# Raw q and k loads moved from SyncE's queue to GpSimd's; three small pieces of work moved in their engines' orders

## The chip, the core and the metric

The kernel runs on one core of a Trainium2 chip (trn2). The metric is the device time in microseconds (us) of one execution; lower is better. The engines are named as the profile names them: PE (TensorE, matmuls), PEld (TensorE's weight loads), DVE (VectorE), ACT (ScalarE), POOL (GpSimd) and SP (SyncE, which only issues DMAs). A "q" behind an engine's name is its sequencer, where DMAs are issued.

## The reference, cut to what matters

```
attention: 4 batches x 8 heads, 576 rows, head_dim 64
  scores = q k^T / 8, causal; plus min(-(cum_i - cum_j), 0), cum = cumsum(max(s, 0))
  x = softmax(scores) v                       -> 2304 tokens x 512
first MLP:   h = max(x w_in, 0);  y = (h*h) w_out      512 -> 2048 -> 512
second MLP:  h = y w_in2;  out = (h cos h) w_out2      512 -> 2048 -> 512
```

The result is wanted in float32. The kernel gets that accuracy from faster formats by splitting a value into a high and a low part and adding three products (high*high, high*low, low*high).

## The kernel before, in words

**Work and stages.** The 2304 tokens of x are cut into 9 blocks of 256 (`NB1`). A block is filled by one or two query segments, each with 8 heads; a head of a segment is a unit of `heads` (96 in all), and its query rows are cut into one or two tiles of up to 128 rows. A tile is a job (160 in all). Units of the early heads (`n < EARLY`, the first 16) take a simpler path. In blocks 3 and 6 the first segment, and in block 8 both, have one tile per head, so every step begins a new head there; elsewhere a head lasts two steps.

The first MLP of block k runs in the same steps as the attention of block k+1. The list `slots` holds its matmul groups in order: (1, chunk) is `g1` (line 857, hidden chunk f of block k: 12 matmuls into `hps`, of which there are two halves), (2, chunk) is `g2` (line 886, 12 matmuls into `y`), two chunks behind. The second MLP comes after the attention, from 612 us on in the trace, and is not touched.

**One step.** `step` (line 990 on) writes out by hand the order in which each engine gets its work. All engines run their own instructions strictly in that order, and wait for each other by semaphores. For step i, with attention and MLP, it is:

1. `x_high`: ACT copies freshly transposed x from PSUM (`xps`) into `xh` (line 668).
2. `load_ext` for the next head (POOL's queue, line 340): the four rows of sums that go under k and q in tile `k2`.
3. The first MLP slot: 12 matmuls. In front of a `g2`, `rests` makes sure that its low part `gl` has been issued (DVE, line 876).
4. `prep_high` (ACT, lines 347 and 348): rounds the raw q and k of the next head into `hi` and `k2`.
5. `evacuate` (DVE): divides a finished pair of heads by their sums into `xp` (line 642).
6. woven together: `softmax_tail` (DVE: mask of tile i-1, line 516; the two halves `p` of tile i-2, lines 561 and 565, then a DMA transpose of `p` on SP, line 571; where the width isn't a multiple of 128, POOL first clears the pad of `p`, line 560), `w_step` (bits of weights) and `v_early` (`v_scale`, lines 405 and 410).
7. `x_low` (DVE, line 674), `rests` (DVE, line 876), `w_lows` (line 750).
8. `act` (ACT, lines 868 to 870): `g` = max(0, h) squared and its high part `gh`.
9. `prep_low` (DVE, lines 355 and 358): the low parts of q and k of the next head. After it the raw tile is free.
10. `emit_qk` (PE, line 502), the other MLP slots, the exponential of tile i-1 (ACT, line 533), `load_v` (SP, line 368).
11. `turn` (PE, line 657): transposes `xp` into `xps`; `v_sums` (PE, line 399); `emit_pv` (PE, line 602).
12. `v_late` (square, high and low parts of v, its load on POOL's queue, its store on SP's), then `load_raw` for the head three ahead (SP, line 221).

**The raw tiles.** `raw` has two buffers. The load for head n waits until `prep_low` of head n-2 has read its buffer, and `prep_high` of head n waits for it to land.

**v.** The values are scaled by a power of two, two heads at a time: 16 groups of `v_load` (line 380), `v_square` (ACT, line 391), `v_sum` (PE: two small matmuls with ones, into other columns of `xps`), `v_scale` (DVE), `v_high` (ACT, line 419), `v_low` (DVE, line 426) and `v_store`. The queue `vq` gives each its step: square in step t, sum in t+1, scale and high in t+2, low and store in t+3. `xps` is one PSUM tile, shared by the sums of v and the transposed x, which lie in different columns.

**Between blocks** there is a step without attention, whose only MLP slot is one group, and then the last x of the block is evacuated and turned. `turn` marks in `xtq` whether a piece is the last of its block.

Of the kernel before, what the change touches and what calls it, by code (L numbers as in the profile page):

```python
# [24 lines left out]
BT = 256  # L25
# [13 lines left out]
def _weave(*chains):  # L39

    chains = [iter(c) for c in chains if c is not None]
    while chains:
        for c in list(chains):
            if next(c, c) is c:
                chains.remove(c)
# [61 lines left out]
DR_BITS = 0  # L107
XST_TO = 20
TURN_FROM = 24
V_STRIDE = 11  # L110
V_NEAR = 6
V_TIME = 7
# [3 lines left out]
def attention_moe_moe_kernel(  # L116
# [18 lines left out]
    nc = tc.nc  # L135
# [59 lines left out]
    for x in range(H // 2):  # L195
        t = wp.tile([128, 2, 2 * BT], F32, tag=f"w{2 * NF - (2, 3, 4, 6)[x]}", name="early")
# [13 lines left out]
    def load_raw(n):  # L210
        nq, nl = heads[n][6], heads[n][8]
        if n < H:
            return
        if n < EARLY:
            t = at.tile([128, KQ], F32, tag=("hi", "k2")[n % 2], bufs=2, name="early1")
            nc.sync.dma_start(out=t[0:64, 0:2 * BT], in_=qk[n, 0:64, 0:2 * BT])
            nc.sync.dma_start(out=t[64:66, 0:2 * BT], in_=c1_d[n - H])
            hd[n] = t
            return
        raw = at.tile([128, KQ], F32, tag="raw", bufs=2, name="raw")  # L220
        nc.sync.dma_start(out=raw[:, BT - nq:BT + nl], in_=qk[n, :, BT - nq:BT + nl])
        hd[n] = [None, None, raw]

    def v_own(b):
# [29 lines left out]
    def store_ones(eng, n0, n1):  # L254
# [10 lines left out]
        out=mask[:, 512:640], in_=mask[:, 512:640], pattern=[[-1, 128]], compare_op=ALU.is_ge,  # L265
# [4 lines left out]
        out=ident, in_=ident, pattern=[[-1, 128]], compare_op=ALU.not_equal, fill=1.0,  # L270
# [3 lines left out]
    for t in early[2:]:  # L274
        early_ones(t, nc.gpsimd)
    nc.vector.tensor_scalar(
        out=cs[0:32, 0:S], in0=cs[0:32, 0:S], scalar1=0.0, scalar2=8.0, op0=ALU.max, op1=ALU.mult
    )
    cc = []
    for x0, x1, t in ((0, BT, "xh"), (BT, S, "xl")):  # L280
        nc.vector.tensor_tensor_scan(
            out=c8[0:32, x0:x1], data0=cs[0:32, x0:x1], data1=cs[0:32, x0:x1],
# [27 lines left out]
    for x in range((XST + 1) // 2):  # L310
        t = wp.tile([128, 2, 512], F32, tag=f"w{2 * NF - 5 - x}", name="xst")
# [18 lines left out]
    evq, xtq, xcq = [], [], []  # L330
# [107 lines left out]
    def v_early():  # L438
        for f, g in vq[0] if vq else ():
            if f is v_scale:  # L440
                yield from f(g)

    def v_sums():
        for f, g in vq[0] if vq else ():
            if f is v_sum:
                f(g)
# [7 lines left out]
    def v_steps(gs, start):  # L454
# [9 lines left out]
        for x, due in enumerate(at):  # L464
            at[x] = max(0, min(due, free))
            free = at[x] + V_STRIDE
        return at

    def v_add(gs, at, stored=True):

        for g, t in zip(gs, at):
            fs = []
            if g not in vs:
                fs, t = [(t, v_load)], t + 2
            fs += [(t, v_square), (t + 1, v_sum), (t + 2, v_scale), (t + 2, v_high), (t + 3, v_low)]
            for x, f in fs + [(t + 3, v_store)] * stored:
                vq.extend([] for _ in range(x + 1 - len(vq)))
                vq[x].append((f, g))
# [171 lines left out]
    def turn(held):  # L650
        while xtq and (held > 0 or xtq[0][-1]):
            held -= 1
            k, c, rws, o, xp, _ = xtq.pop(0)
            pt = xps[:, 0:BT]
            m = 0
            for ti, r in enumerate(rws):
                nc.tensor.transpose(pt[:, m:m + r], xp[0:r, ti, :], ident[0:r, 0:r])  # L657
                m += r
            xcq.append((k, c, o, m, pt))

    def x_high():
        for k, c, o, m, pt in xcq:
            if k not in xb:
                xb[k] = (
                    m1.tile([128, KD, BT], F32R, tag="xh", bufs=2, name="xh"),
                    m1.tile([128, KD, BT], F32R, tag="xl", bufs=2, name="xl"),
                )
            nc.scalar.copy(xb[k][0][:, c, o:o + m], pt[:, 0:m])

    def x_low():  # L670
        while xcq:
            k, c, o, m, pt = xcq.pop(0)
            xh, xl = xb[k]
            nc.vector.tensor_tensor(  # L674
                out=xl[:, c, o:o + m], in0=pt[:, 0:m], in1=xh[:, c, o:o + m], op=ALU.subtract
            )
# [3 lines left out]
    nraw, next_, nhigh, nlow = [2], [0], [0], [0]  # L680

    def upto(cnt, n, f):
        while cnt[0] < min(n, NH):
            f(cnt[0])
            cnt[0] += 1

    def job(i):
        return jobs[i] if 0 <= i < NJ else None
# [4 lines left out]
    def heads_ahead(i, *fs):  # L693
        if job(i) and jobs[i][1] == 0:
            for cnt, f, d in fs:
                upto(cnt, jobs[i][0] + d, f)
# [263 lines left out]
    g2done = [0]  # L960
# [6 lines left out]
    def moe_slot():  # L967
        part, n = slots.pop(0)
        k, f = chunks[n]
        if part == 1:  # L970
            w_need(2 * f + 1)
            g1(k, f)
            return n
        w_need(2 * f + 2)
        rests(n)
        g2(k, f)
        g2done[0] += 1
        if k == NB1 - 1 and 2 * f >= RAWS:
            w_load(2 * (NF + f))
            w_load(2 * (NF + f) + 1)  # L980
            nw[0] = max(nw[0], 2 * (NF + f + 1))
# [14 lines left out]
    def softmax_tail(i):  # L996
        if job(i - 1):
            yield from emit_mask(i - 1)
        for j in stage(2, i - 2):
            yield from emit_split(j)  # L1000

    def step(moe=0, bits=0, attn=True):

        i = prog[0]
        held = len(xtq)
        prog[0] += attn
        if attn:
            for j in stage(1, i - 2):
                emit_exp(j)
        x_high()  # L1010
        if attn and job(i - 2):
            emit_turn(i - 2)
        if attn:
            heads_ahead(i, (next_, load_ext, 2))
        w_age()
        w_scales()
        n = moe_slot() if moe else None
        if attn:
            heads_ahead(i, (nhigh, prep_high, 2))
        _weave(evacuate())  # L1020
        y_evict()
        if not attn:
            rests()
        _weave(softmax_tail(i) if attn else None, w_step(bits), v_early())
        x_low()
        rests()
        w_lows()
        if attn and job(i - 1) and jobs[i - 1][0] < EARLY:
            for j in stage(1, i - 1):
                emit_exp(j)  # L1030
        act(n)
        if attn:
            heads_ahead(i, (nlow, prep_low, 2))
        if attn and job(i):
            emit_qk(i)
        for _ in range(moe - 1):
            act(moe_slot())
            y_evict()
        w_sums()
        if attn:  # L1040
            for j in stage(1, i - 1):
                emit_exp(j)
        if attn:
            for j in stage(0, i - 2):
                if jobs[j][1] == 0:
                    load_v(jobs[j][0])
        turn(held if moe and i > last_job[0] + TURN_FROM else len(xtq))
        v_sums()
        if attn:
            for j in stage(3, i - LAG[0]):  # L1050
                if j > i - lag(j):
                    stages[3] -= 1
                    break
                emit_pv(j)
        w_ahead()
        v_late()
        if attn:
            heads_ahead(i, (nraw, load_raw, 4))
        if later and prog[0] >= later[0][0]:
            later.pop(0)[1]()  # L1060

# [17 lines left out]
    def w_age():  # L1079
        wsum.extend(wsq)  # L1080
        wsq.clear()
# [18 lines left out]
    def w_lows():  # L1100
        while wlow:
            w_lo(wlow.pop(0))

    def w_step(n):

        js = list(range(nw[2], min(nw[2] + n, wlim[0])))
        while wlow:
            w_lo(wlow.pop(0))
            yield
        w_squares()  # L1110
        while wrest:
            w_rest(wrest.pop(0))
        if js:
            w_clip_to(js[-1])
            for _ in zip(*[w_bits(j) for j in js]):
                yield
            for j in js:
                if wq[j][0] == 0:
                    wrest.append(j)
                else:  # L1120
                    wbit.append(j)
            nw[2] += len(js)
# [18 lines left out]
    def w_need(j):  # L1141

        w_stats(j)
        while wrest and wrest[0] < j:
            w_rest(wrest.pop(0))
        while wlow and wlow[0] < j:
            w_lo(wlow.pop(0))
# [10 lines left out]
    while prog[0] < unit_done(0):  # L1158
        i = prog[0]
# [3 lines left out]
    for k in range(NB1):  # L1163
# [6 lines left out]
        last = len(slots) - nslots  # L1170
        J = goal - start + 1 if goal > start else NF
        for i in range(J):
            bits = 0
            if k == 0:
# [3 lines left out]
                bits = int((i + 1) * B0_BITS) - int(i * B0_BITS)  # L1178
            if k == NB1 - 1:
# [16 lines left out]
                bits = min(2 * GROUPS[0][1], int(max(0, i - 1) * B8_BITS)) - int(max(0, i - 2) * B8_BITS)  # L1196
                bits = max(0, bits)
            n = len(slots) - last - nslots + math.ceil(nslots * (i + 1) / J)
# [233 lines left out]
```

## Time and profile before

| | |
|---|---|
| median of 3 runs | 996.22 us (994.47 to 996.5) |
| the profiled execution, its own time | 994.47 us |
| its span, first to last instruction | 992.7 us |
| attention and first MLP | 0 to 612 us of the span |
| second MLP | 612 us to the end |
| PE busy over the span | 960.4 us (97%) |
| DVE, ACT, POOL busy | 729.7, 654.2, 162.7 us |

A row of the profile's timeline reads: start in us from the span's start, duration in us, engine, line, operation, output tile <- input tiles, shapes, count; in brackets the idle time of the engine just before, and the instruction or DMA that ended it.

### The profile page before, as it was taken

Reading aid. Unit: us, or ns where it says so; the run is one execution under the profiler, and the core shown is the slowest. Engines: PE = TensorE matmul, PEld = TensorE weight load, DVE = VectorE, ACT = ScalarE, POOL = GpSimd, SP = SyncE. Lnnn points to the kernel's source line nnn. Section 1 sums busy time; section 2 is a strip of 40 time slices with the busy share of each in tenths; the row PEclk is TensorE's granted clock in tenths of the full one; section 3 lists DMA queues with packets and bytes.
Section 4 is the critical chain, followed back from the end, with each engine's and each line's share of the span. In section 5 each row is a group of like instructions: output and inputs, shape, how many; then the busy total and the mean of one; then the engine's idle time right before and its main releaser. Section 6 shows DMA issues by size and latency. Waiting matters only on the chain.

```text
span 992.7 us, 20523 instructions
## 1 busy us (share of the span) xinstructions
PE 960.4 (97%) x7266; PEld 737.9 (74%) x7266; DVE 729.7 (74%) x1865; ACT 654.2 (66%) x1596; POOL 162.7 (16%) x258
## 2 busy tenths in 40 slices
PE   5999899999999999999999999999999999999998
PEld 4788898899999999999999997444444454444444
DVE  6979788878777897777988265898988855545555
ACT  4789776777768777766776586677766543334333
POOL 2000011111111121111110023421043440001101
PEclk9999999999999999999999999999999999999999
DMA  7955589756877886467898579210000000001001
GB/s 262 307 179 182 128 199 204 169 124 161 190 173 163 181 193 169 119 143 156 191 214 177 193 240 357 90 39 1 1 1 1 1 1 1 11 33 43 30 14 64
DMA packets 150711, 126.65 MB, mean 128 GB/s; under 512 B 108048, under 2 KB 125792, under 8 KB 150608
## 3 DMA queue, kind: packets, MB, share of 16 engines
q1 hardware_dynamic: 146688, 119.05, 45.9%
q0 software_dynamic: 3904, 6.29, 2.4%
q8 instruction: 57, 0.93, 0.4%
q14 instruction: 46, 0.38, 0.1%
q10 hardware_dynamic: 16, 0.01, 0.0%
HBM read 85.25 MB, written 15.81 MB: 102 GB/s over the span
## 4 chain that ended last, share of the span: by engine, by line
PE 83%; DVE 8%; ACT 4%; DMA 2%; issue 2%; SPq 0%; DVEq 0%; ACTq 0%
PE hps L857 19%; PE y L886 18%; PE o L1310 18%; PE hp L1255 18%; PE qkp L502 4%; PE pvs L602 4%; DVE wt L750 1%; DMA raw<-in_qk_dram 1%; DVE st L729 1%; DVE sb L516 1%; PE xps L657 1%; ACT sb L533 1%; DMA early<-c 1%; DMA rw<-in_w_dram 0%; DVE k L358 0%
## 5 line engine op out<-in xcount | busy, mean ns | idle before, releaser
L857 PE MATMUL hps<-xh,wt 128*128 128x256 f32 x1152 | 239.5, 291 | 4.1 <-ACT g L868 4.0
L886 PE MATMUL y<-gh,wt 128*128 128x256 f32 x1152 | 236.6, 288 | 0.0
L857 PEld LDWEIGHTS hps<-xh,wt 128*128 128x128 f32 x1152 | 190.2, 192 | 6.6 <-ACT g L868 5.4
L886 PEld LDWEIGHTS y<-gh,wt 128*128 128x128 f32 x1152 | 188.8, 191 | 1.2
L1255 PE MATMUL hp<-yh,wt 128*128 128x512 f16 (+1 forms) x640 | 185.9, 358 | 0.0
L1310 PE MATMUL o<-wt,gh 128*128 128x512 f16 x576 | 171.3, 379 | 1.5 <-ACT wt L1325 1.4
L886 PE MATMUL y<-gl,wt 128*128 128x256 f32 x576 | 162.9, 283 | 1.6 <-DVE gl L876 1.6
L857 PE MATMUL hps<-xl,wt 128*128 128x256 f32 x576 | 163.5, 284 | 0.9 <-DVE xl L674 0.9
L1255 PEld LDWEIGHTS <-wt 128*128 128x128 f16 x960 | 91.9, 98 | 93.0
L1267 ACT ACTIVATE a<-hp,hsc 128x512 f32<-128x512 f32 (+1 forms) x80 | 51.4, 643 | 115.9 <-PE hp L1255 114.5
L868 ACT ACTIVATE g<-hps 128x256 f32<-128x256 f32 x144 | 54.6, 379 | 104.8 <-PE hps L857 103.2
L1255 PE MATMUL hp<-yl,wt 128*128 128x512 f16 (+1 forms) x320 | 114.4, 358 | 0.0
L886 PEld LDWEIGHTS y<-gl,wt 128*128 128x128 f32 x576 | 110.0, 191 | 2.7 <-DVE gl L876 2.2
L857 PEld LDWEIGHTS hps<-xl,wt 128*128 128x128 f32 x576 | 110.8, 192 | 1.4 <-DVE xl L674 1.1
L1310 PE MATMUL o<-wt,gl 128*128 128x512 f16 x288 | 109.2, 379 | 0.0
L1268 DVE TENSOR_SCALAR kf<-a 128x512 f32<-128x512 f32 (+1 forms) x80 | 35.0, 437 | 96.4 <-ACT a L1267 95.7
L1310 PEld LDWEIGHTS <-gh 128*128 128x128 f16 x576 | 56.3, 98 | 66.3 <-issue 1.7
L533 ACT ACTIVATE sb<-sb,nb 128x128 f32<-128x128 f32 (+8 forms) x160 | 93.8, 586 | 11.8 <-DVE nb L516 11.7
L340 POOL DMA_DIRECT2D k<-ext_d x80 | 41.1, 513 | 338.1 <-ACT g L869 103.7
L516 DVE CUSTOM_DVE_ANT_0 sb<-qkp,mask 128x128 f32<-128x128 f32 (+8 forms) x160 | 72.7, 454 | 13.3 <-PE qkp L493 6.9
L1276 ACT ACTIVATE a<-kf 128x512 f32<-128x512 f32 (+1 forms) x80 | 46.8, 585 | 48.3 <-DVE kf L1269 47.8
L876 DVE TENSOR_TENSOR gl<-g,gh 128x256 fp32r<-128x256 f32 x144 | 60.9, 423 | 21.6 <-PE y L886 11.3
(119 smaller groups left out, 1694.8 us busy)
## 6 DMA issues: line engine op xcount, KB each, us to landing
rw<-in_w_dram SPq DMA_DIRECT2D x64, 512.0 KB
raw<-in_qk_dram SPq DMA_DIRECT2D x32, 352.0 KB
raw<-in_qk_dram SPq DMA_DIRECT2D x16, 384.0 KB
v_d<-vt SPq DMA_DIRECT2D x16, 320.0 KB
raw<-in_qk_dram SPq DMA_DIRECT2D x16, 320.0 KB
vb<-v_d SPq DMA_DIRECT2D x32, 160.0 KB
vr<-in_v_dram POOLq DMA_DIRECT2D x15, 320.0 KB, 4.6
y_d<-yst SPq DMA_DIRECT2D x18, 256.0 KB
```

What stands on the lines that cost most here:

```text
L340: nc.gpsimd.dma_start(out=hd[n][1][64:68, BT - nq:BT + nl], in_=ext_d[n, :, BT - nq:BT + nl])
L502: nc.tensor.matmul(p[0:r, 0:cn], m[0:kk, qo:qo + r], m[0:kk, BT + c0:BT + c0 + cn], start=(kk == 128), stop=(kk == 68),)
L516: nc.vector.tensor_tensor_reduce(out=sb[0:r, c0:c0 + cn], in0=p[0:r, 0:cn], in1=mask[0:r, mo + c0:mo + c0 + cn], scale=-0.125, scalar=(3.0 ...
L533: nc.scalar.activation(out=sb[0:r, 0:w], in_=sb[0:r, 0:w], func=ACTF.Exp, scale=-1.0, bias=j["nb"], accum_out=pd[n - h % 2]["z"][0:r, ti, ...
L857: nc.tensor.matmul(hp, w[:, a, c * 128:(c + 1) * 128], (xh, xl)[e][:, c, :], start=(n == 0), stop=(n == 3 * KD - 1),)
L868: nc.scalar.activation(out=g, in_=hp, func=ACTF.Relu)
L876: nc.vector.tensor_tensor(out=gl, in0=g, in1=gh, op=ALU.subtract)
L886: nc.tensor.matmul(yps[k][d // 2][:, d % 2, :], w[:, a, d * 128:(d + 1) * 128], (gh, gl)[e], start=(f == 0 and n == 0 and d % 2 == 0), sto ...
L1255: nc.tensor.matmul(hp, w[:, a, c * 128:(c + 1) * 128], (yh, yl)[e][:, c, :], start=(m == 0), stop=(m == 3 * KD - 1),)
L1267: nc.scalar.activation(out=a, in_=hp, func=ACTF.Copy, scale=sm["hsc"][:, j, f:f + 1], bias=0.25)
L1276: nc.scalar.activation(out=a, in_=kf, func=ACTF.Sin, scale=-6.2831850)
L1310: nc.tensor.matmul(ops[j][a], (gh, gl)[e][:, a * 128:(a + 1) * 128], w[:, x, :], start=(first and m == 0), stop=(last and m == 2),)
```

## The change

- `load_raw` issues on POOL's queue (line 221). Up to step 27 it stays at the step's end; later the same load stands at the start of the next step, just behind `load_ext`. 80 loads are concerned.
- `v_sum` goes to entry t+2 of `vq`, and `v_sums()` stands behind the first MLP slot of a step, no longer between `turn` and `emit_pv`. So the two matmuls of a group move from the end of one step to behind the first group of matmuls of the next.
- `v_early()` (`v_scale`) leaves the woven part and follows `prep_low`.
- While fewer than two `g2` are done, `rests()` is called ahead of `softmax_tail` in steps with attention, too.
- Where the last piece of a block has been turned, `x_low` is called ahead of `softmax_tail`; `turn` passes on the mark for it.

```diff
+RAW_LATE = 28
...
-        nc.sync.dma_start(out=raw[:, BT - nq:BT + nl], in_=qk[n, :, BT - nq:BT + nl])
+        nc.gpsimd.dma_start(out=raw[:, BT - nq:BT + nl], in_=qk[n, :, BT - nq:BT + nl])
...
-            fs += [(t, v_square), (t + 1, v_sum), (t + 2, v_scale), (t + 2, v_high), (t + 3, v_low)]
+            fs += [(t, v_square), (t + 2, v_sum), (t + 2, v_scale), (t + 2, v_high), (t + 3, v_low)]
...
-            k, c, rws, o, xp, _ = xtq.pop(0)
+            k, c, rws, o, xp, last = xtq.pop(0)
...
-            xcq.append((k, c, o, m, pt))
+            xcq.append((k, c, o, m, pt, last))
...
             heads_ahead(i, (next_, load_ext, 2))
+            if i > RAW_LATE:
+                heads_ahead(i - 1, (nraw, load_raw, 4))
         w_age()
         w_scales()
         n = moe_slot() if moe else None
+        v_sums()
...
         y_evict()
-        if not attn:
+        if not attn or g2done[0] < 2:
             rests()
-        _weave(softmax_tail(i) if attn else None, w_step(bits), v_early())
+        done = bool(xcq) and xcq[-1][-1]
+        if done:
+            x_low()
+        _weave(softmax_tail(i) if attn else None, w_step(bits))
         x_low()
...
             heads_ahead(i, (nlow, prep_low, 2))
+        _weave(v_early())
         if attn and job(i):
             emit_qk(i)
...
         turn(held if moe and i > last_job[0] + TURN_FROM else len(xtq))
-        v_sums()
...
         v_late()
         if attn:
-            heads_ahead(i, (nraw, load_raw, 4))
+            if i < RAW_LATE:
+                heads_ahead(i, (nraw, load_raw, 4))
```

## Rows read from the trace of the kernel before

**Rows 1.** The page's first part: busy us (share of the span) and instructions.
```profile
PE 960.4 (97%) x7266; PEld 737.9 (74%) x7266; DVE 729.7 (74%) x1865; ACT 654.2 (66%) x1596; POOL 162.7 (16%) x258
```
**Rows 2.** Timeline of PE: six waits, each with what ended it.
```profile
57.20 0.38 PE L886 MATMUL y<-gl,wt 128*128 128x256 f32 x1 [1.62 <-DVE gl L876]
...
113.79 0.39 PE L857 MATMUL hps<-xl,wt 128*128 128x256 f32 x1 [0.88 <-DVE xl L674]
...
117.27 0.27 PE L399 MATMUL xps<-ss,ones 128*128 128x2 f32 x1 [1.55 <-ACT vt L391]
...
173.13 0.39 PE L857 MATMUL hps<-xh,wt 128*128 128x256 f32 x1 [1.10 <-ACT g L868]
...
183.67 0.27 PE L657 MATMUL xps<-ident,xp 64*128 64x64 f32 x1 [0.54 <-DVE vsc L405]
...
517.27 0.39 PE L857 MATMUL hps<-xh,wt 128*128 128x256 f32 x1 [1.66 <-ACT g L868]
```
**Rows 3.** Timelines of ACT near 57 us and of DVE near 112 us.
```profile
57.24 0.39 ACT L868 ACTIVATE g<-hps 128x256 f32<-128x256 f32 x1 [1.28 <-DVE gl L876]
...
111.84 0.68 DVE L516 CUSTOM_DVE_ANT_0 sb<-qkp,mask 128x512 f32<-128x512 f32 x1
```
**Rows 4.** ACT's waits for raw: who <- whom: us, times, longest; two in the timeline.
```profile
ACT hi L347 <- DMA raw<-in_qk_dram: 15.4, 11, 4.7
...
171.93 0.72 ACT L347 CAST hi<-raw 128x640 fp32r<-128x640 f32 x1 [4.70 <-DMA raw<-in_qk_dram]
...
515.96 0.78 ACT L347 CAST hi<-raw 128x704 fp32r<-128x704 f32 x1 [3.67 <-DMA raw<-in_qk_dram]
```
**Rows 5.** The chain of waits: those raws, issue and us to landing; DVE freeing their buffers.
```profile
166.42 5.43 DMA raw<-in_qk_dram
...
511.01 4.87 DMA raw<-in_qk_dram
...
163.56 0.75 DVE L358 TENSOR_TENSOR k<-raw,hi 64x576 fp32r<-64x576 f32 x1
...
506.56 0.75 DVE L358 TENSOR_TENSOR k<-raw,hi 64x576 fp32r<-64x576 f32 x1
```
**Rows 6.** Line 380, POOL's loads of v: ns min/median/max, landing; POOL and DVE near 170 us.
```profile
L380 POOL DMA_DIRECT2D vr<-in_v_dram x15: 735/752/779, 75.3 to 386.7; - x15
...
DMA to landing us min/median/max: 3.3/4.6/5.9
...
170.74 0.51 POOL L340 DMA_DIRECT2D k<-ext_d  x1 [3.35 <-DVE p L561]
...
170.28 0.45 DVE L561 TENSOR_SCALAR p<-sb 64x576 f16<-64x576 f32 x1
```
**Rows 7.** PE's turns in three steps, DVE's work there, v_scale's group of the lines view.
```profile
202.40 0.27 PE L657 MATMUL xps<-ident,xp 64*128 64x64 f32 x1
...
218.06 0.48 PE L657 MATMUL xps<-ident,xp 128*128 128x128 f32 x2
...
246.40 0.27 PE L657 MATMUL xps<-ident,xp 128*128 128x128 f32 x1
...
202.99 0.42 DVE L358 TENSOR_TENSOR k<-raw,hi 64x256 fp32r<-64x256 f32 x1
...
219.34 0.42 DVE L358 TENSOR_TENSOR k<-raw,hi 64x256 fp32r<-64x256 f32 x1
...
247.14 0.42 DVE L876 TENSOR_TENSOR gl<-g,gh 128x256 fp32r<-128x256 f32 x1
...
L405 DVE TENSOR_SCALAR vsc<-xps 128x2 int32<-128x2 int32 x16 | 2.5, 154 | 5.5 <-PE xps L399 3.4 <-ACT xh L668 2.1
```
**Rows 8.** POOL at the start; a window: us, busy by engine, PEclk, DMA share, GB/s.
```profile
5.56 0.52 POOL L192 MEMSET early<- 2x512 f32 x1
...
8.00:9.00 1.00, 0.00 (x0) 0.00 (x0) 0.00 (x0) 0.00 (x0) 0.00 (x0) 1.00 0.28 105
```
**Rows 9.** The page's group of ACT's first reading of hps (idle before, and its releaser).
```profile
L868 ACT ACTIVATE g<-hps 128x256 f32<-128x256 f32 x144 | 54.6, 379 | 104.8 <-PE hps L857 103.2
```

More of the change, by code (lines that the diff above doesn't have):

```diff
@@ L658, in turn @@
                 m += r
-            xcq.append((k, c, o, m, pt))
+            xcq.append((k, c, o, m, pt, last))
     def x_high():
-        for k, c, o, m, pt in xcq:
+        for k, c, o, m, pt, _ in xcq:
             if k not in xb:
@@ L671, in x_low @@
         while xcq:
-            k, c, o, m, pt = xcq.pop(0)
+            k, c, o, m, pt, _ = xcq.pop(0)
             xh, xl = xb[k]
```

## Prediction

> **What bounds the kernel now.** I read the page first, then PE's waits in its timeline, then what the releasers of those waits were doing on their own engines. The page says that PE is busy 97% of the span [rows 1]: 992.7 less 960.4 leaves 32.3 us in which it does nothing. That is all a change of order can win, and most of it lies where this change doesn't reach (the start before the first matmul, the prolog). So the prediction is a list of single waits of PE, each about 1 us, and the reader is to see in [rows 2] which engine ended each. DVE and ACT have idle time on the whole [rows 1], so their lateness counts only where PE stands waiting for exactly that operation.
>
> **The change part by part.** 0.2% of this kernel is 2.0 us, about what a measurement can tell from no change.
>
> *First low parts.* `rests()` goes ahead of `softmax_tail` for the first two `g2`. It moves DVE's `gl`, one operation per chunk; no DMA moves. PE stood 1.62 us for the first at 57.20 [rows 2]. ACT stood 1.28 us for the same `gl`, because it could not write the next `g` before the old one was read [rows 3]. With `gl` earlier both waits go, and the next thing late is ACT itself, so I take ACT's 1.28; bounds 0 and 1.62. The mask moved behind `gl` has no price, as ACT has its own work ahead of the exponential that follows.
>
> *A block's last x.* `x_low`, one DVE operation, goes ahead of the mask that started at 111.84 [rows 3], and PE stood 0.88 us for it at 113.79 [rows 2], from 112.91 on. Started in the mask's place it ends before PE gets there: 0.88; bounds 0 and 0.88. The other blocks show no such wait, and get nothing. The mask comes later by one short operation that runs beside PE's matmuls.
>
> *v's sums on PE.* Two small matmuls for each of 16 groups. One waited 1.55 us for ACT's squares, in the short step between two blocks at 117.27 [rows 2]. Behind the next step's first group of matmuls the squares are done: 1.55 is won; bounds 0 and 1.55.
>
> *v_scale on DVE, the price.* Two operations, 0.15 us each [rows 7], now come last of DVE's work in their step. Who waits for them? The row at 183.67 shows PE's `turn` standing for `v_scale` [rows 2]: it writes other columns of `xps`, yet it has to wait until `v_scale` has read. So in each step that holds a `v_scale` and a `turn`, PE now waits for all DVE work of that step. Counting steps from the loops, there are three such steps with attention where DVE is the later one (a fourth has two MLP slots ahead of its `turn`, and DVE is done by then). In the first, DVE's last piece ends at 202.99 + 0.42 = 203.41; less 0.30 for the two operations that no longer stand ahead of it, plus 0.15 for the first of them, `v_scale` has read at 203.25, where `turn` started at 202.40: 0.85 lost. In the second, 219.34 + 0.42 - 0.15 = 219.60 against 218.06: 1.55 (about; DVE there waits for ACT's exponential, so nothing ahead of it gets earlier). In the third, without `prep_low`, 247.14 + 0.42 - 0.15 = 247.40 against 246.40: 1.00 [rows 7]. Together 3.4 us, and PE has no idle time near by to take them up; bounds 0 and 4.5, should DVE be a third of a microsecond later in each. Queued behind the waiting `turn` are `emit_pv` and the next step's matmuls.
>
> *Raw loads.* 80 DMAs of up to 384 KB leave SP's queue and stand on POOL's. On SP each stood behind the step's DMA transpose, the load of vb and the store of v; on POOL it stands behind the sums' rows (`load_ext`), which are short. ACT waited 11 times for a raw, 15.4 us in all [rows 4], but only two of those waits were long enough to reach PE, through a late `g`: 4.70 us of ACT gave 1.10 of PE at 173.13, and 3.67 gave 1.66 at 517.27 [rows 2, 4]. Their buffers were free at 163.56 + 0.75 = 164.31 and 506.56 + 0.75 = 507.31, and SP issued them at 166.42 and 511.01 [rows 5]: 2.1 and 3.7 us late. POOL can issue them at once. From issue to landing SP's two took 5.43 and 4.87 us [rows 5]; POOL's loads of v, 320 KB, take 4.6 us, at worst 5.9 [rows 6]. Even with 5.9 the two land 1.6 and 2.7 us sooner. ACT's first wait then shrinks to about 3.1, under the 4.70 - 1.10 = 3.60 that cost PE nothing; the second to about 1.0, under 3.67 - 1.66 = 2.0. I take both in full, 2.76; bounds -4 (they land later, below) and 2.76.
>
> What now queues behind a raw on POOL: while it waits for `prep_low`, the pad of `p`, the next sums' rows and the load of v stand, and DVE's `p` and SP's transpose wait for the pad. A raw's issue costs POOL about 0.75 us, as the loads of v [rows 6]; so the pad is done about 1 us behind `prep_low`, and DVE gets to `p` about a mask later, 0.68 [rows 3]. A few tenths of DVE here and there: 0 to 1, and I take 0.3.
>
> The first raw moves most. POOL's work at the start ends at 5.56 + 0.52 = 6.08 [rows 8], and nothing that this raw needs is missing then, so it is loaded at 6 us instead of 79, amid the loads that PE's first matmul waits for. DMA is only 0.28 busy from 8 us on, at 105 GB/s [rows 8]; at that rate per busy share 384 KB take about 1.0 us. Bounds 0 and 1.0; I take 0.3, nearer the idle window.
>
> [...] The row at 170.74 shows POOL's DMA beginning as DVE's `p` ended (170.28 + 0.45) [rows 6]: an issue on POOL can be held by DVE, up to 0.45 us here. [...]
>
> *The sum.* Won: 1.28 + 0.88 + 1.55 + 2.76 = 6.47. Lost: 3.4 + 0.3 + 0.3 = 4.0. Net 2.5 us. The profiled execution took 994.47 us with a span of 992.7; it becomes 992.0. That execution was the fastest of three, and the median is 1.75 above it, so for the median I take 996.2 - 2.5 = 993.7 us.
>
> **The rivals.**
>
> - *The turns don't wait.* If DVE gets to `v_scale` before PE gets to `turn`, the 3.4 us stay away: 996.2 - 5.9 = 990.3. For it: DVE loses its own waits for the sums, 5.5 us over the 16 groups [rows 7]. Against: in the second of the three steps DVE is held by ACT, not by the sum. Chance 0.18.
> - *The small waits come back.* PE gets past 57, 113 and 117 us sooner and then meets the same ACT and DVE, so 1.28 + 0.88 + 1.55 are given back: 996.2 - 2.76 + 4.0 = 997.4, no change. For it: ACT and DVE are tightest there. Against: ACT and DVE get part of the time, too. Chance 0.17.
> - *v_scale is late for ACT, too (slower).* `v_high` comes in the same step on ACT, which then stands with `prep_high` and `g` behind it. If at the other 13 groups it waits the 1.13 us that the three turns wait on average, and half reaches PE, that is 7.4: 996.2 - 2.5 + 7.4 = 1001.1. It decides from where ACT's wait exceeds its idle time ahead of `g`. Against: ACT waits 103.2 us for `hps` there in 144 times [rows 9], 0.7 each, on the whole. Chance 0.14.
> - *Raws land later (slower).* POOL's issue is held by DVE time and again, and raws land 1.5 us later than now instead of sooner. The two long waits then grow by 1.5 each, and cost PE 3.0 more on top of the 2.76 not won; the other nine, 0.8 us each today, grow to 2.3, where PE begins to feel it: 1.0 in all. 996.2 - 2.5 + 2.76 + 4.0 = 1000.5. It decides where landing takes over 7.5 us from when the buffer is free. Against: POOL's slowest was 5.9 [rows 6]. Chance 0.09. [...]
>
> **How the numbers follow.** The forecast keeps 0.42, with a range of its own from 991.5 to 996. Six tenths of it lie beyond 2.0 us: 0.25, and with the first rival 0.43 for faster. The rest of it, and most of the second rival, give 0.32 for within 0.2%. The last two and a little of the second give 0.25 for slower. The range runs from 989.8 to 999.8: below lies a part of the first rival, above the upper half of the slower ones, about 0.2 together.
>
> **What would show it.** Right: PE's waits for `gl` at 57, `xl` at 113 and ACT's squares at 117 are gone; ACT's waits for raw fall from 15.4 to a few us; PE's waits at `turn` for `vsc` grow from one of 0.54 to four with some 4 us; POOL shows 80 more DMAs of about 0.75 us, the first near 6 us. Wrong: no `turn` waiting for `vsc` (first rival), new waits of PE for `g` behind `v_high` (third), ACT's waits for raw above 15.4 us (fourth), or a first matmul that starts later than now.

## The result: 1.1% slower, and the profile after

The changed kernel takes 1005.96 us (median of 6 executions, 1000.95 to 1014.64) where the kernel before, on the same chips, takes 995.87 (993.96 to 996.63): a ratio of 1.0108, with a 95% interval of 1.0083 to 1.0133. The forecast was 993.7 with a range up to 999.8. The profiled execution took 1007.27 us, its span is 1005.5 us, 12.8 more than before.

PE's row of the page of the changed kernel:

```profile
PE 966.2 (96%) x7266; PEld 742.0 (74%) x7266; DVE 731.6 (73%) x1865; ACT 655.9 (65%) x1596; POOL 211.5 (21%) x338
```

Against [rows 1], PE is busy 5.8 us longer for the same 7266 matmuls, and stands idle 7.0 us more (1005.5 - 966.2 = 39.3 against 32.3). So the loss has two halves, waits and slower matmuls. PE's timeline of the changed kernel, its new or longer waits:

```profile
94.38 0.38 PE L400 MATMUL xps<-ss,ones 128*128 128x2 f32 x2 [0.80 <-ACT xh L669]
...
169.20 0.39 PE L858 MATMUL hps<-xh,wt 128*128 128x256 f32 x1 [1.12 <-ACT g L869]
...
176.52 0.34 PE L503 MATMUL qkp<-hi 128*64 128x288 f32 x1 [2.09 <-DVE nb L517]
...
203.41 0.27 PE L658 MATMUL xps<-ident,xp 64*128 64x64 f32 x1 [2.09 <-DVE vsc L406]
...
222.43 0.54 PE L658 MATMUL xps<-ident,xp 128*128 128x128 f32 x2 [1.58 <-DVE vsc L406]
...
252.10 0.53 PE L658 MATMUL xps<-ident,xp 128*128 128x128 f32 x2 [1.01 <-DVE vsc L406]
...
532.54 0.38 PE L858 MATMUL hps<-xh,wt 128*128 128x256 f32 x1 [3.44 <-ACT g L869]
```

The waits at 57, 113 and 117 us of [rows 2] are gone, as forecast. Their 4.05 us are outweighed by others: `turn` waits for `vsc` (5.1 us with a fourth wait of 0.42), qk waits for the mask's `nb` (4.2 us in 5 waits, where before had one of 0.21 us), and `g` is late twice for a raw. The windows of the same execution show the second half:

```profile
core 0: us, PE busy (x) PEld busy (x) DVE busy (x) ACT busy (x) POOL busy (x), PEclk, DMA share, GB/s
...
178.00:181.00 3.00, 3.00 (x25) 2.71 (x24) 2.00 (x7) 1.98 (x5) 0.78 (x2) 0.50 0.06 12
...
205.00:209.00 4.00, 4.00 (x25) 3.80 (x24) 2.31 (x8) 2.31 (x7) 1.27 (x2) 0.57 0.49 112
...
533.00:536.00 3.00, 3.00 (x16) 3.00 (x15) 2.66 (x8) 1.72 (x4) 0.79 (x2) 0.50 1.10 228
```

Behind each of its three longest waits after the first matmul (2.09, 2.09 and 3.44 us) PE is granted half its clock (PEclk 0.50, 0.57 and 0.50 above), and the matmuls of 256 columns start 0.21 us apart in place of 0.12 (at 178.08 and 176.84). Each such stretch lasts 3.41 us in the clock's record. At half speed that loses 1.7 us, an estimate from this length, and 5.1 us in all, near the 5.8 us by which PE is busy longer. Before's record, which begins at 52 us, has none until its last microseconds (PEclk 0.50 from 991.0 us on, when PE has no matmul left). 7.0 + 5.1 is nearly all of the 12.8.

### The profile page after: what moved, and what is told of

It reads as the page before. It is cut to its first block, busy times and chain, and to the rows that moved or that the text cites. A ratio compares the mean times of both kernels' runs of the same rounds, so it can differ in the third digit from the quotient of the medians.

```text
span 1005.5 us, 20434 instructions
## 1 busy us (share of the span) xinstructions
PE 966.2 (96%) x7266; PEld 742.0 (74%) x7266; DVE 731.6 (73%) x1865; ACT 655.9 (65%) x1596; POOL 211.5 (21%) x338
## 4 chain that ended last, share of the span: by engine, by line
PE 75%; DVE 9%; ACT 6%; DMA 6%; issue 3%; SPq 0%; DVEq 0%; ACTq 0%; POOLq 0%
PE o L1318 18%; PE hp L1263 18%; PE hps L858 16%; PE y L887 15%; PE qkp L503 4%; PE pvs L603 3%; DMA raw<-in_qk_dram 3%; DMA rw<-in_w_dram 2%; ACT sb L534 1%; DVE sb L517 1%; DVE wt L751 1%; DVE st L730 1%; PE xps L658 1%; DVE k L359 1%; DMA pt<-p 1%
## 5 line engine op out<-in xcount | busy, mean ns | idle before, releaser
L222 POOL DMA_DIRECT2D raw<-in_qk_dram x80 | 45.9, 574 | 253.6 <-ACT gh L871 65.9
```

The costliest lines, as they stand in the source:

```text
L222: nc.gpsimd.dma_start(out=raw[:, BT - nq:BT + nl], in_=qk[n, :, BT - nq:BT + nl])
```

## The experiments

Ratios are to the kernel before, run beside it, with 95% intervals. The diffs are against the kernel before where nothing else is said.

**Run e1_gl_xl: the two moves on DVE alone.**

```
+        if not attn or g2done[0] < 2:
             rests()
+        done = bool(xcq) and xcq[-1][-1]
+        if done:
+            x_low()
         _weave(softmax_tail(i) if attn else None, w_step(bits), v_early())
```

> The kernel before with only the first low parts and the block's last x low moved. Theory A (these two edits do what they say, and the loss of 10 us is elsewhere): PE's waits at 57 and 113 us go and nothing takes their place, 995.9 - 1.28 - 0.88 = 993.7 us. Rival (the waits come back a few microseconds later, on ACT or DVE): 995.9 us, with new PE waits of some 2 us in all before 130 us. Rival (the loss comes from here): over 998 us.

Ratio 0.9993 (0.9982 to 1.0004), no difference that can be told. The waits at 57 and 113 us are gone, but new ones of qk for `nb` stand at 177 (1.11 us), 368 (0.52) and 496 (0.79): 2.42 us, about what the two had won (1.62 + 0.88). They aren't a few microseconds later, as the first rival said, but at later blocks' ends. DVE's timeline there:

```profile
176.68 0.42 DVE L674 TENSOR_TENSOR xl<-xps,xh 128x256 fp32r<-128x256 f32 x1 [0.68 <-ACT xh L668]
177.02 0.44 DVE L516 CUSTOM_DVE_ANT_0 sb<-qkp,mask 64x288 f32<-64x288 f32 x1
```

DVE stands in `xl` 0.68 us for ACT's `xh`, which ACT writes at 176.29, behind an exponential (174.62) and two squares of v (175.39, 175.84). The mask stands behind `xl`, and PE's next qk stood 1.11 us until the mask had read its buffer.

**Run e2_raw_only: the raws on POOL alone.**

```
-        nc.sync.dma_start(out=raw[...], in_=qk[...])
+        nc.gpsimd.dma_start(out=raw[...], in_=qk[...])
         heads_ahead(i, (next_, load_ext, 2))
+        if i > RAW_LATE:
+            heads_ahead(i - 1, (nraw, load_raw, 4))
```

> The kernel before with only the raw loads moved to GpSimd's queue, behind the sums' rows. Theory A (the raws are issued sooner, 0.55 us after the buffer is free instead of some 2, but take longer to land, 4.4 us on the mean and up to 9 in the stretch from 490 to 535 us, so that PE waits there for g): the two waits of 1.10 and 1.66 do not go, one of some 3.4 us comes with a stretch at half clock behind it (1.7 us), 995.9 + 3 = 999 us, between 997 and 1001. Rival (as predicted, the two waits go): 993.1 us. Rival (the raws alone make the whole loss): 1006 us.

Ratio 1.0014 (0.9995 to 1.0032): at the lower end of theory A, and not told apart from no change. The spread is wide, 994.3 to 1003.0 us over 12 executions; the five above 998 all had a granted clock of 0.996 or less. In the profiled one (1000.29 us) PE's wait at 173 us is gone, the one near 517 stays (1.44 at 516), and this came, on ACT and PE, and in the windows of the same execution half a clock for 7 us:

```profile
523.40 0.78 ACT L348 CAST hi<-raw 128x704 fp32r<-128x704 f32 x1 [5.29 <-DMA raw<-in_qk_dram]
...
524.71 0.58 PE L858 MATMUL hps<-xh,wt 128*128 128x256 f32 x1 [4.23 <-ACT g L869]
```

```profile
523.00:530.00 7.00, 5.29 (x24) 5.29 (x25) 3.79 (x10) 3.86 (x10) 1.29 (x3) 0.51 1.14 184
```

**Run e3_v_only: the moves on v alone.**

```
-    (t + 1, v_sum)
+    (t + 2, v_sum)
         n = moe_slot() if moe else None
+        v_sums()
-        _weave(softmax_tail(i) if attn else None, w_step(bits), v_early())
+        _weave(softmax_tail(i) if attn else None, w_step(bits))
             heads_ahead(i, (nlow, prep_low, 2))
+        _weave(v_early())
         turn(...)
-        v_sums()
```

> The kernel before with only the work on v moved (v's sums on PE behind the next step's first slot, v_scale and its companions last of DVE's and ACT's work in the step). Theory A (PE's turn waits for v_scale in four steps, and two of the waits are long enough that PE's clock falls behind them): 995.9 - 1.55 + (5.1 - 0.54) + 2 x 1.7 = 1002.3 us, and PE's waits at turn for vsc stand at some 5 us. Rival (as predicted, the waits at turn cost 3.4 and no clock): 997.8 us. Rival (the waits at turn come only with the raws on GpSimd): 994.3 us.

Ratio 1.0049 (1.0031 to 1.0067), between theory A and the prediction's own terms (3.4 - 1.55 lost). The waits at `turn` are 0.42, 0.85, 1.58 and 1.01 us. Two half-clock stretches stand in its profile, one behind the 1.58, one behind the old wait of 1.62 for `gl`.

**Run e4_raw_on_sp: the changed kernel with the raws back on SP.**

```
-        nc.gpsimd.dma_start(out=raw[...], in_=qk[...])
+        nc.sync.dma_start(out=raw[...], in_=qk[...])
```

> The changed kernel with only the raw loads put back on SP's queue. Theory A (raws cost some 3 us, the rest is v's): 1006.0 - 3 - 1 = 1002 us at most, with no wait of 3.4 us for g near 532 us and no half clock there, while the turns' waits for vsc stay at some 5 us. Rival (raws do no harm, as predicted): 1006 us plus 2.8. Rival (raws make the whole loss): 993 us.

Ratio 1.0052 (1.0036 to 1.0069): the raws cost 5.6 per mille in the changed kernel, and 1.4 alone. Here qk waits 1.10 us for `nb` at 177 in place of 2.09, `turn` 1.47 at 202 in place of 2.09, and one half-clock stretch is left.

**Runs e5_gl_only and e6_xl_only: e1's two parts.** Each has its hunk of e1's diff and not the other.

> The kernel before with only the first low parts moved ahead of the mask. Theory A (this edit wins what I gave it, and what it and the x edit won together was spent by the x edit later on): the wait of 1.62 us at 57 us goes, and no wait of qk for nb comes at 177 us; 995.7 - 1.3 to 1.6 = 994.2 us. Rival (the time comes back within a few steps because ACT and DVE are behind): 995.7 us and new waits of over 1 us in all between 57 and 180 us.

> The kernel before with only a block's last x low moved ahead of the mask. Theory A (in the later blocks DVE stands in x low for ACT's xh, the mask behind it starts late, and PE's next qk waits for the mask's nb): the wait of 0.88 us at 113 us goes, waits of qk for nb come at some 177, 370 and 500 us, 1.11 + 0.52 + 0.79 = 2.4 us as in the run of both edits; 995.7 + 1.5 = 997.2 us. Rival (those waits came from the phase of the step, shifted by the first low parts): 994.8 us and no such waits.

The first low parts: 0.9990 (0.9977 to 1.0003), no wait in place of the 1.62. `x_low`: 1.0024 (1.0014 to 1.0034), slower, with the waits of 1.11, 0.52 and 0.79 us where e1 has them. The waits are as theory A had them in both, and e6's time, too; e5's time isn't told apart from no change.

**Run e7_v_scale_back: v's sums moved on PE, v_scale left beside the mask.** It is e3 without its two `v_early` lines.

> The kernel before with v's sums moved on PE behind the next step's first slot, but with v_scale and its companions left in their place beside the mask. Theory A (the turns wait for v_scale because it is last of DVE's work, not because the sums are late): the four waits at turn for vsc shrink to the 0.54 us of before or less, the 1.55 us at 117 us go, a wait of 0.8 us for xh near 95 us and one of 0.4 near 300 stay; 995.7 - 1.55 + 1.2 = 995.3 us. Rival (DVE now stands in the middle of its work for PE's sum, and the turns and the mask are as late): 1000 us.

Ratio 1.0010 (0.9999 to 1.0021). Of the four waits at `turn` 0.42 us is left, so it is `v_scale`'s place that makes them: 3.9 per mille between e3 and e7. For the sums' own move no gain can be told. The 1.55 us at 117 go, and in the waits' table stands this, two waits of 0.80 and 0.40 us:

```profile
PE xps L399 <- ACT xh L668: 1.2, 2, 0.8
```

At its new place the sum comes before ACT has read the transposed x out of `xps`, and although the sum writes other columns of the tile, PE waits for that reading.

**Run e8_raw_on_act: the raws on ACT's queue.**

```
-        nc.sync.dma_start(out=raw[...], in_=qk[...])
+        nc.scalar.dma_start(out=raw[...], in_=qk[...])
```

(and placed as in e2.)

> The kernel before with the raw loads on ACT's queue in place of GpSimd's, at the same place in the step. Theory A (what hurts is that raw's packets go through the DMA engines at the same time as the transposes' packets of 256 bytes, where on SP they came behind them): as on GpSimd, the transposes' issue in the stretch from 480 to 540 us takes 1.8 to 2.2 us on the mean in place of 1.41, raws land late there and PE waits 2 to 4 us for g; about 998 to 1001 us, ACT's own issues among it. [...]

Ratio 1.0020 (1.0006 to 1.0033). In the profiled execution the raws came sooner: ACT's waits for them fell from 15.4 to 8.4 us, PE's at 173 and 517 are gone, one of 1.68 came at 528. The transposes from 480 to 540 us took 1.46 us each to issue on the mean (1.41 before, 2.24 in e2). So raws that travel beside the transposes need not slow them, against theory A. That they do on POOL's queue (2.24 us) points to POOL's path, but no run shows which part of it is slow. The time is longer than before all the same. Of the 2.7 us by which this profile's span (995.4 us) is longer, 1.7 fit the stretch at half clock at 118 us, behind the wait of 1.55 us for `vt` that before has, too; so about 1.0 us is left in it for ACT's issues.

**Run e9_after_scale_back: the changed kernel with v_scale back beside the mask** (`v_early()` again the third of the woven pieces).

> The changed kernel with v_scale and its companions put back beside the mask; v's sums stay behind the first slot and the raws on GpSimd. Theory A (the place of v_scale costs as much here as it did alone, 3.9 us, and more where late transposes hold DVE's p, as at 203 us): the four waits at turn fall from 5.1 us to under 1, the half clock at 205 us goes, 1006.0 - 4.2 - 1.7 = 1000 us. Rival (DVE's time is full, and the waits go elsewhere): 1004 us or more.

Ratio 1.0063 (1.0038 to 1.0087), 4.5 per mille better than the changed kernel: nearer theory A (5.9) than its rival (2 at most). The profile shows 0.42 us at `turn`, as theory A said; it still has waits of 2.31 for `nb` at 175 and of 3.48 and 3.14 for `g` at 521 and 530, where one raw took 13.5 us to land, and a stretch at half clock for each of the three.

**Run e10_raw_pool_to_86: raws on POOL up to head 85 only.**

```
-        nc.sync.dma_start(out=raw[...], in_=qk[...])
+        (nc.gpsimd if n < 86 else nc.sync).dma_start(out=raw[...], in_=qk[...])
```

> The kernel before with the raws on GpSimd's queue for the heads up to 85 and on SP's from 86 on (from about 485 us). Theory A (the raws on GpSimd hurt only in the dense last stretch of the attention, where every step needs a new raw): the wait of 4.2 us at 524 us is gone, the wait of 1.10 us at 173 stays away; 994.7 - 1.1 = 993.6 us, and a narrow spread. Rival (they hurt all along, by transposes that land late): 996 to 997 us as with all raws on GpSimd.

Ratio 1.0012 (0.9997 to 1.0027), inconclusive: the wait at 524 is gone and the one at 173 is 0.49, as theory A wanted, but the executions spread from 992.7 to 999.6 us. The narrow spread did not come.

**Runs e11_best and e12_best_raw: the three waits repaired otherwise.** e11 has e1's diff, with two changes; e12 adds the raws of e10.

```
+        done = bool(xcq) and xcq[-1][-1] and xcq[-1][0] == 1
-            v_add(gs, v_steps(gs, start))
+            at_ = v_steps(gs, start)
+            at_[2] += 1
+            v_add(gs, at_)
```

`x_low` goes ahead of the mask only at the end of the one block where PE waited for it, and the third group of v comes a whole step later, in its old order.

> The kernel before with the first low parts moved, with x low ahead of the mask in the one block where PE waited for it, and with the third group of v moved by one whole step in place of the order of PE's and DVE's work. Theory A (each of the three waits was real and can go without a new one): no waits at 57, 113 and 117 us and none of qk for nb at 177, 370 and 500; 994.7 - 1.0 - 0.88 - 1.55 = 991.3 us. Rival (PE comes sooner and meets the same ACT and DVE): 994 us.

> The kernel of the three repaired waits with the raws on GpSimd's queue for the heads up to 85. Theory A (both gains add): 991.3 - 1.1 = 990.2 us. Rival (the raws on GpSimd take back what the rest wins): 993 us or more.

e11: 989.17 us, ratio 0.9954 (0.9930 to 0.9978); e12: 988.50 us, 0.9940 (0.9925 to 0.9955). Both beat both kernels. e11's gain of 4.6 per mille is larger than the forecast 3.4 us, but its interval holds that, too. Between e11 and e12 no difference can be told, so a gain from the raws isn't shown. PE's waits in e11:

```profile
PE hps L857 <- ACT g L868: 2.9, 7, 0.8
...
PE xps L657 <- DVE vsc L405: 0.5, 1, 0.5
```

No `gl`, `xl`, `vt` or long `nb` is left. PE's waits of over 0.15 us sum to 22.6 us against 27.9 before: besides the three, one of 0.47 us at 125 is gone and the one near 517 is halved. e11's profile holds no half-clock stretch; in before's executions beside it the mean clock lies between 0.996 and 1.000, so some of those may have had one, which no trace here shows.

**Runs e13_after_raw_sp_86 and e14_after_xl_one: two parts taken out of the changed kernel.**

```
-        nc.gpsimd.dma_start(out=raw[...], in_=qk[...])
+        (nc.gpsimd if n < 86 else nc.sync).dma_start(out=raw[...], in_=qk[...])
```

```
-        done = bool(xcq) and xcq[-1][-1]
+        done = bool(xcq) and xcq[-1][-1] and xcq[-1][0] == 1
```

> The changed kernel with the raws back on SP's queue from head 86 on (from about 485 us), and on GpSimd's before that. Theory A (the raws cost 5.6 us in the changed kernel, 1.0108 less 1.0052, and most of it in the dense last stretch, by the wait of 3.44 us for g and the half clock behind it): 1006 - 3.44 - 1.7 + 0.9 = 1001.8 us, a ratio to before of about 1.0060, and no execution above 1005. Rival (they cost as much before 485 us, by late transposes): 1004 us or more, a ratio of 1.0085 or more.

> The changed kernel with x low ahead of the mask only in the block where PE waited for it. Theory A (x low ahead of the mask in the later blocks takes 2.09 + 0.56 + 0.52 + 0.79 = 4.0 us of PE's waits for nb and one half clock at 177 us, 1.7, and leaves less slack for the raws behind it): 1006 - 4 to 5.7 = 1000.3 to 1002 us, a ratio of 1.0045 to 1.0062. Rival (it costs what it cost alone, 1.0024 + the 0.88 us it won): 1002.7 us, a ratio of 1.0075. Rival (the later blocks' waits go elsewhere): 1006 us.

e13: 1.0078 (1.0059 to 1.0097). It lies between the two theories: by the ratios, of the raws' 5.6 per mille about half is lost after 485 us (3.0) and half before (2.6), with intervals as wide as these parts. No execution was above 1005 us, as theory A said. e14: 1.0032 (1.0015 to 1.0049), below theory A's lower end of 1.0045, which its interval holds. Without `x_low` ahead of the later blocks' masks the changed kernel gets back 7.6 per mille, the most that any single part gave. Its waits for `nb`:

```profile
PE qkp L503 <- DVE nb L517: 0.8, 2, 0.6
```

`nb` falls from 4.2 to 0.8 us, and `turn`'s wait at 200 us from 2.09 to 0.84, as in e3 (0.85). The profile has no half-clock stretch until its last microseconds.

## Why the prediction was wrong, step by step

*A block's last x: the step that failed.* The prediction gave `x_low` 0.88 won, "the other blocks show no such wait, and get nothing", and "the mask comes later by one short operation that runs beside PE's matmuls". The 0.88 is won, but the mask is not late by one operation of 0.4 us: it is late by what DVE waits for `xh`. In the changed kernel:

```profile
175.29 0.35 ACT L669 CAST xh<-xps 128x256 fp32r<-128x256 f32 x1
```

```profile
173.27 0.75 DVE L359 TENSOR_TENSOR k<-raw,hi 64x576 fp32r<-64x576 f32 x1
175.68 0.42 DVE L675 TENSOR_TENSOR xl<-xps,xh 128x256 fp32r<-128x256 f32 x1 [1.66 <-ACT xh L669]
176.02 0.44 DVE L517 CUSTOM_DVE_ANT_0 sb<-qkp,mask 64x288 f32<-64x288 f32 x1
```

1.66 us of waiting, then 0.34 for `xl` itself: the mask is 2.0 us late, and PE stood 2.09. I checked what the moved operation does for its own waiter in every block, not what it waits for in every block. The table of waits of before already showed DVE waiting so, and in the changed kernel it waits twice as long:

```profile
DVE xl L674 <- ACT xh L668: 5.3, 5, 2.6
```

```profile
DVE xl L675 <- ACT xh L669: 11.5, 11, 2.6
```

With the 0.88 us won in it, the move costs 2.4 per mille alone (e6), and in the changed kernel taking it out of the later blocks gives back 7.6 (e14).

*v_scale: right in place and size, but not in price.* The three waits were forecast as 0.85, 1.55 and 1.00; e3 shows 0.85, 1.58 and 1.01. The price of 3.4 us left out the half clock (in e3 one stretch stands behind the 1.58), and that in the changed kernel the first grows to 2.09, with such a stretch behind it. Taken back it gives 3.9 (e7 against e3) or 4.5 per mille (e9). The first rival, that the turns don't wait, is refuted.

*v's sums.* The 1.55 are won, but two new waits for `xh` (0.80 and 0.40) were not forecast, and e7's ratio of 1.0010 shows no gain. In the timeline of before the sum at 180.54 stood 0.24 us for `xl`, which could have told that they meet in `xps`.

*Raw loads: the gain of 2.76 isn't there.* The first half, that they are issued sooner, was right. In the changed kernel each raw from the third on was issued 0.55 to 0.57 us after its buffer came free (2.1 on the mean before). The bound on landing wasn't:

```profile
DMA to landing us min/median/max: 2.8/3.9/9.3
```

The bound of 5.9 came from the 15 loads of v. In the last stretch, where each step of some 4 us needs a raw, the rows of sums behind the raws in POOL's queue took up to 8.4 us to land (5.1 before) and SP's transposes 1.77 us each to issue (1.41 before). One raw issued at 526.11 landed 9.24 us later, and 11 KB of sums issued at 523.01 took 8.4. ACT waited 16.7 us for raws in all, where a fall from 15.4 to a few us was forecast; with the raws back on SP (e4) it waited 10.2. PE's wait of 1.10 at 173 stayed (1.12 at 169). In that stretch the fourth rival had the time of landing right, down to its bound of 7.5 us, but not on the whole: alone, the raws cost 1.4 per mille (not told apart from 0). The 0.3 us put down for the pads of `p` isn't seen: DVE waited 9.5 us for them, 10.6 before.

*A hold by DVE.* The hold that I read from the row at 170.74 [rows 6] isn't one. That issue starts 0.51 us behind the end of PE's last reading of the same kind of tile:

```profile
169.93 0.30 PE L502 MATMUL qkp<-k 68*64 68x288 f32 x1
```

So do 69 of the 80 issues of line 340 in that trace, and 72 of the 80 start while some DVE operation is running, 7 of them within line 561 itself. In the changed kernel all 80 issues of raws took 0.54 to 0.72 us, so no hold shows in the issue. ACT waits 8.4 us for raws on ACT's queue (e8) and 18.2 on POOL's (e2), but no run here shows DVE as the cause; what happens between the issue and the first packet stays open.

*First low parts; start; v_high.* e5 has the wait of 1.62 gone and a ratio of 0.9990, consistent with the 1.28 given but not told apart from 0. The first raw went out at 6.7 us, and the first matmul started at 9.33 as before: 0, not 0.3. ACT's waits for `vsc` rose to 8.0 us, as the third rival said, but in e3, where only v's work was moved, no new wait of PE for `g` stands near them (there ACT waited 5.8). The second rival, that the small waits come back, is refuted by e11, whose profile has PE waiting 5.2 us less in all.

*The sum.* Alone the parts make -1.0 (e5) + 2.4 (e6) + 4.9 (e3) + 1.4 (e2) = 7.7 per mille; together they make 10.8. Taken out of the changed kernel one by one, `x_low` gives 7.6, the raws 5.6 and `v_scale` 4.5, 17.7 in all. They don't add, in part because taking out either of two parts gives back the same loss: of the three stretches at half clock (5.1 us) e4's profile has one left and e14's none, though e9's still has three. The rest of the overlap isn't accounted for. The wait at 203 is 0.84 with the raws on POOL and `x_low` in its old place in that block (e14), 1.47 with `x_low` moved and the raws on SP (e4), 2.09 with both. In the changed kernel DVE stands there for a transpose of `p` to land, and all that follows up to `v_scale` is late:

```profile
201.56 0.23 DVE L562 TENSOR_SCALAR p<-sb 128x128 f16<-128x128 f32 x1 [2.52 <-DMA pt<-p]
```

In e14 the same wait is 1.35 us. Why that transpose comes later with `x_low` moved was not traced.

## What to carry to other kernels

Before an operation is moved ahead of another on its engine, look at what it waits for at every place where it runs: here its wait became the wait of all that then stood behind it (1.66 us of DVE for `xh`, then 2.09 of PE for `nb`). When PE is 97% busy, a repair is best confined to the one place where the trace shows the wait (e11: three local repairs, 0.9954). In these traces two uses of one PSUM tile waited for each other even in different columns (`turn` for `v_scale`, up to 2.09 us, the sums for `xh`, up to 0.80), so count every reader of the tile when one is moved.

## What the runs showed of the hardware that was not expected

A wait of PE can cost more than its length, when its clock falls behind it. In the profiles, stretches at half clock of 3.41 us (once twice that, around the end of the 4.23 us in e2) began near the end of or behind waits of 1.47 (e4), 1.55 (e6, e8), 1.56 (e5), 1.58 and 1.62 (e3), 2.00 (e13), 2.09 and 3.44 us (the changed kernel), and 2.31, 3.14 and 3.48 us (e9); half of 3.41 is 1.7 us lost. But it isn't a fixed rule for a wait: in the profile of before, waits of 1.55, 1.62 and 1.66 us [rows 2] were followed by none, nor were one of 1.58 us in the changed kernel, at 222 us, and one of 2.35 us in e14, at 525 us. The granted clock varies from one execution of a kernel to another, too: the mean clock of before's executions beside e11 lay between 0.996 and 1.000. A prediction for a kernel this full should price a wait of 1.5 us at 1.5 to 3.2, an estimate from these waits and the 1.7.
